# A local-attention and gated-MLP kernel: load order, mask split and written order of its first part

## Chip, cores and metric

The kernel runs on one core of a Trainium2 chip. The metric is the device time of one execution in microseconds (us), the median of several. The core has five engines that each work through a fixed list of instructions: PE (TensorE, with its weight loads listed as PEld), ACT (ScalarE), DVE (VectorE), POOL (GpSimd) and SP (SyncE, which here only issues DMAs). They wait for each other through semaphores.

## What is computed

Attention over 8 batches, 8 heads, 576 positions and 64 channels, in which a query sees 32 keys (the heads of the lower half: the last 32 positions; the others: every fourth of the last 128). Its result, as 4608 tokens of 512 channels, goes through a gated MLP of width 1536. All in float32.

```python
    mask_plain = (rel >= 0) & (rel < window)
    mask_dil = (rel >= 0) & (rel < window * dilation) & (rel % dilation == 0)
    scores = np.where(masks[None, :, :, :], scores, -1000000000.0)
    attn = np.exp(scores - max); attn = attn / (sum + 1e-09)
    x = (attn @ v).transpose(0, 2, 1, 3).reshape(B * S, H * D)
    g = x @ w_gate
    silu = g * (1.0 / (1.0 + np.exp(-g)))
    val = x @ w_val
    return (silu * val @ w_out)
```

## The kernel before

**Two kinds of work.** The tokens are cut into chunks. For the first four chunks of 384 tokens the MLP is done "plain": 12 blocks f of the width 1536 per chunk, and each block is a gate product (`bg`, 12 matmuls of 128x384), a value product (`bv`, 12) and, one block later, the output product (`bo`, 12). Each number is held as a high and a low float32r part, so that a product of 512 channels takes 4 x 3 matmuls, three for the products of the parts. The remaining tokens are done later by another scheme (pieces, line 777), which the change does not touch.

**Packs.** The attention of one chunk and one pair of heads is a pack. Chunk 0 needs packs 0 to 3, all ahead of the first gate product. The stages of a pack have one-letter names in the written order: Q scores on PE (mask by a matmul with the identity, lines 348 and 354), S maximum and subtraction on DVE (368, 369), X exponential on ACT (374), T transposition on PE (378), K copy to SBUF on ACT (384), A products with v on PE (394), N normalisation on DVE (403 to 405), U transposition on PE (412), H high part of x on ACT (444), L low part of x on DVE (448). Packs 4 and on are attended between the products, by a table of slots.

**Weight units.** The weights come as 24 units of 768 KB (two for each f), packed as 64-bit numbers, and each unit passes five stages, written `W0` to `W4`: E on ACT (235), T (253 on ACT or 256 on DVE, as `by_act` says), B on DVE (263 or 266; both read two operands from SBUF), H on ACT (274), L on GpSimd (278). A unit must pass all five before PE can use all of it. The raw units lie in six places, so `w_load` can load a seventh only when B of the first is done.

**Order.** For the first chunk's packs a string of letters sets the order of PE, DVE and ACT word for word (`Y2` is two matmuls that compute nothing and keep PE running, `M` issues two more loads). Behind it the scheduler of the language orders the loop `for s in range(NS)`, in which block s calls the gate product, tanh on ACT (468), a product on DVE (473), the value product, a second product on DVE (478), the high part on ACT (483), the output product of block s-1, and the low part on GpSimd (488). The PSUM banks of the first part are given back before the loop, and `bg` and `bv` take those of `bank_x` and `bank_k`.

**Loads.** SP issues most loads, ACT the masks, pack 1's q and k, and later all v. Each queue issues in the order of the code. The loads take eight semaphores in turn, so a load waits until the one eight places ahead of it has landed.

Of the kernel before, what the change touches and what calls it, by code (L numbers as in the profile page):

```python
# [18 lines left out]
P = 128  # L19
# [116 lines left out]
def attention_moe(ctx, tc, qkb, vb, w, masks, ident, out):  # L136
# [49 lines left out]
    consts = at(0, (NM * BK + P) // 2, BF16)  # L186
    mask_sb, ident16 = consts[:, :NM * BK], consts[:, NM * BK:]

# [5 lines left out]

    WARM = 9
    wt = [at(M_W + 2 * WU * u, 2 * WU, F32R) for u in range(NU)]
# [42 lines left out]
    def by_act(u):  # L239
        return u in (1, 2) or u > 3 and u % 2 == 1  # L240

# [78 lines left out]
    for k, fn, fb in (("qk", FQ, 4), ("v", 4 * FG * (D + 1), 3), ("e", P * FG, 2), ("y", P * FG, 2), ("pt", P * FG, 2)):  # L320
        step = -(-fn // 8) * 8
        early[k] = Ring(fn, *range(o, o + step * fb, step))
        o += step * fb
# [4 lines left out]
    def load_qk(m, pool, engine):  # L328
        t = pool["qk"]()
        engine.dma_start(out=t[:, :pk(m).cols], in_=qkb[m, :, :pk(m).cols])  # L330
        st[m]["qk"] = t
# [184 lines left out]

    bank_x, bank_k, bank_r, *s_banks = [bank(ab, *x) for x in (("fx", 1), ("fk", 1), ("fr", 2), ("fs0", 2), ("fs1", 2))]


    load_qk(0, fa, nc.sync)  # L520
    nc.scalar.dma_start(out=consts, in_=masks)
    load_qk(1, fa, nc.scalar)
    load_v(0, fa, nc.sync)
    nc.sync.dma_start(out=idents, in_=ident.rearrange("n p c -> p n c"))
    nc.vector.memset(ones, 1.0)
# [10 lines left out]

    idle(WARM)
    load_qk(2, fa, nc.sync)
    load_v(1, fa, nc.sync)
    w_load()  # L540
    load_qk(3, fa, nc.sync)
    load_v(2, fa, nc.sync)
    w_load()

    def more_in():
        load_v(3, fa, nc.sync)
        w_load()
        ready["w"] = True

# [6 lines left out]
        "U": lambda m: turn_y(m, x_bank[m]), "H": lambda m: x_copy_hi(m, x_bank[m]),  # L556
        "L": lambda m: x_copy_lo(m, x_bank[m]), "M": lambda m: more_in(), "Y": idle, "W": lambda n: w_one(STAGES[n]),
    }

    et = mybir.EngineType  # L560
    with tc.manual_schedule(engines={et.PE, et.DVE, et.Activation}):
        for what in ("Q0 Q1 Y2 S0 X0 T0 Y2 S1 K0 X1 A0 M0 W0 Q2 N0 T1 K1 S2 X2 Q3 W1 W0 S3 X3 A1 U0 N1 W2 T2 K2 H0 L0 W3 W4 "
                     "T3 A2 K3 W1 U1 N2 A3 H1 L1 W0 W2 U2 N3 W3 H2 U3 L2 W4 H3 L3 W1 W0 W2 W1 W2 W3 W0 W0").split():
            first[what[0]](int(what[1]))
# [33 lines left out]
    def attend(now):  # L598
        what, m = visit.get(now, ("", 0))
        if what == "A":  # L600
            if m > 4:
                results(m - 1, two)
            if m < NPK:
                scores(m, two, m < 8)
            if m > 4:
                norm(m - 1, two, later)
            if m < NPK:
                shift(m, two, later, m < 8)
                exps(m)
                load_v(m, later, nc.scalar)  # L610
                if m + 1 < NPK:
                    load_qk(m + 1, later, nc.scalar)
        elif what == "B":
            if m > 4:
                turn_y(m - 1, two[:, 0])
            if m < NPK:
                turn_e(m, two[:, 1])
                keys(m, two[:, 1], later)
            if m > 4:
                x_copies(m - 1, two[:, 0])  # L620
# [287 lines left out]
def layout(q, k, v, moe_w_gate, moe_w_val, moe_w_out):  # L908
# [17 lines left out]
    w = np.ascontiguousarray(w.reshape(NF, P, 2, WU).transpose(0, 2, 1, 3))  # L926
    masks = np.concatenate([block_masks(), np.eye(P)], axis=1).astype(ml_dtypes.bfloat16)
    order = np.arange(P).reshape(DIL, BQ).T.ravel()
# [21 lines left out]
```

## Time and profile before

| | us |
|---|---|
| median of 3 runs (946.07 to 946.78) | 946.75 |
| the profiled execution | 947.04 |
| its span, first to last instruction | 945.3 |
| PE busy in the span | 929.0 |
| ACT, DVE, POOL busy | 391.9, 633.3, 345.9 |

The prediction is made against the profiled execution, whose span is 945.3 us and whose time is 947.04 us. The trace is read by rows of a timeline: start, length, engine, line, operation, what it writes and reads, how many in a row, and in brackets how long the engine sat idle ahead of it and what ended that. An `x12` row is twelve instructions with no idle time between them. PE's rows overlap, since matmuls are pipelined.

### The profile page before, as it was taken

What the parts mean: (1) busy time and instruction counts of PE and PEld (TensorE: products, weight loads), DVE (VectorE), ACT (ScalarE), POOL (GpSimd) and SP (SyncE); (2) the same over time, 40 slices, a digit from 0 to 9 for tenths busy, and PEclk for the clock granted to TensorE, in tenths of its full rate; (3) what the DMA queues carried; (4) which work ended last, traced back from release to release, by engine and by line L of the source; (5) the groups of instructions that cost most, each with busy time, mean ns of one, the idle gap of its engine ahead of it and who ended that gap; (6) DMA issues with size and microseconds to landing.
All of it is one profiled execution on the core that took longest, in us unless ns stands there. A gap on an engine that the chain in (4) does not pass through costs nothing.

```text
span 945.3 us, 21894 instructions
## 1 busy us (share of the span) xinstructions
PE 929.0 (98%) x9193; PEld 810.9 (86%) x9193; DVE 633.3 (67%) x1008; ACT 391.9 (41%) x687; POOL 345.9 (37%) x364
## 2 busy tenths in 40 slices
PE   7899999999999999999999999999999999999998
PEld 4799999999999999888888788888887888888886
DVE  4767566676677865666568984666689845656882
ACT  4885323233233334343344553343355523334352
POOL 0765421111111131224245672232257723344481
PEclk9999999999999999999999999999999999999999
DMA  9985156577767791776667678776764786655573
GB/s 371 330 282 202 36 200 204 189 235 238 237 196 236 244 324 39 226 245 205 227 205 258 202 241 260 229 235 199 254 203 162 232 256 192 198 185 176 177 249 107
DMA packets 75249, 205.25 MB, mean 217 GB/s; under 512 B 7568, under 2 KB 23824, under 8 KB 75152
## 3 DMA queue, kind: packets, MB, share of 16 engines
q0 software_dynamic: 27216, 99.10, 33.4%
q1 hardware_dynamic: 35696, 65.07, 19.3%
q10 hardware_dynamic: 12240, 39.70, 12.7%
q8 instruction: 72, 1.18, 0.5%
q14 instruction: 25, 0.20, 0.1%
HBM read 161.37 MB, written 42.47 MB: 216 GB/s over the span
## 4 chain that ended last, share of the span: by engine, by line
PE 91%; DVE 4%; DMA 2%; ACT 2%; issue 1%; ACTq 0%; DVEq 0%
PE bo L777 30%; PE bg L777 11%; PE bv L777 11%; PE bo L496 10%; PE bv L459 10%; PE bg L459 10%; PE two L394 3%; PE two L354 2%; PE two L378 2%; DVE at_float L740 2%; PE two L412 1%; DMA at_int<-w 1%; DMA at_float<-qkb 1%; ACT at_float32r L274 0%; DVE at_float L805 0%
## 5 line engine op out<-in xcount | busy, mean ns | idle before, releaser
L777 PE MATMUL bo<-at_float32r 128*128 128x512 f32 x1296 | 308.0, 391 | 0.0
L777 PEld LDWEIGHTS bo<-at_float32r 128*128 128x128 f32 x1296 | 242.1, 188 | 51.6 <-ACT at_float L503 0.2
L706 POOL DMA_DIRECT2D at_float32r<-pieces x189 | 103.5, 548 | 249.7 <-PE bo L777 147.0
L740 DVE TENSOR_TENSOR at_float<-bo,at_float 128x512 f32<-128x512 f32 x168 | 113.8, 686 | 109.6 <-ACT at_float L782 59.8
L488 POOL TENSOR_TENSOR at_float32r<-at_float,at_float32r 128x384 fp32r<-128x384 f32 x48 | 55.4, 1154 | 219.7 <-PE bo L496 179.7
L777 PE MATMUL bv<-at_float32r 128*128 128x512 f32 x486 | 129.7, 393 | 0.0
L777 PE MATMUL bg<-at_float32r 128*128 128x512 f32 x486 | 129.6, 393 | 0.0
L740 DVE TENSOR_TENSOR at_float32r<-at_float,at_float32r 128x512 fp32r<-128x512 f32 (+1 forms) x84 | 99.2, 1205 | 40.5 <-ACT at_float32r L767 24.9
L459 PE MATMUL bg<-at_float32r,at_float32r 128*128 128x384 f32 x576 | 110.9, 339 | 2.1 <-DVE at_float L473 1.3
L740 POOL TENSOR_TENSOR at_float32r<-at_float,at_float32r 128x512 fp32r<-128x512 f32 x63 | 96.4, 1532 | 44.7 <-ACT at_float32r L767 43.3
L459 PE MATMUL bv<-at_float32r,at_float32r 128*128 128x384 f32 x576 | 110.6, 339 | 0.0
L496 PE MATMUL bo<-at_float32r,at_float32r 128*128 128x384 f32 x576 | 110.1, 338 | 0.0
L777 PEld LDWEIGHTS bv<-at_float32r 128*128 128x128 f32 x486 | 90.1, 188 | 19.3
L777 PEld LDWEIGHTS bg<-at_float32r 128*128 128x128 f32 x486 | 90.2, 188 | 19.0 <-DVE at_float32r L740 0.2
L767 ACT CAST at_float32r<-at_float 128x512 fp32r<-128x512 f32 x126 | 76.2, 622 | 68.1 <-PE bv L777 23.2
L459 PEld LDWEIGHTS bg<-at_float32r,at_float32r 128*128 128x128 f32 x576 | 100.0, 188 | 3.8 <-POOL at_float32r L278 1.1
L496 PEld LDWEIGHTS bo<-at_float32r,at_float32r 128*128 128x128 f32 x576 | 100.2, 188 | 0.9
L459 PEld LDWEIGHTS bv<-at_float32r,at_float32r 128*128 128x128 f32 x576 | 100.0, 188 | 1.0 <-DVE at_float L478 0.3
L803 ACT ACTIVATE at_float<-at_float 128x512 f32<-128x512 f32 x72 | 45.6, 633 | 85.4 <-DVE at_float L740 85.2
L473 DVE SCALAR_TENSOR_TENSOR at_float<-at_float,bg 128x384 f32<-128x384 f32 x48 | 26.6, 553 | 76.7 <-ACT at_float L468 76.7
L782 ACT COPY at_float<-bg 128x512 f32<-128x512 f32 x63 | 36.9, 586 | 86.2 <-PE bg L777 86.1
L278 POOL TENSOR_TENSOR at_float32r<-at_int,at_float32r 128x768 fp32r<-128x768 f32 x24 | 45.8, 1916 | 41.5 <-ACT at_float32r L274 41.3
(80 smaller groups left out, 966.3 us busy)
## 6 DMA issues: line engine op xcount, KB each, us to landing
at_float32r<-pieces POOLq DMA_DIRECT2D x189, 512.0 KB, 4.5
pieces<-at_float32r SPq DMA_DIRECT2D x126, 256.0 KB, 4.8
at_int<-w SPq DMA_DIRECT2D x24, 768.0 KB, 6.9
at_float<-vb ACTq DMA_DIRECT2D x28, 390.0 KB, 4.6
at_float<-vb ACTq DMA_DIRECT2D x14, 520.0 KB, 5.5
at_float<-qkb ACTq DMA_DIRECT2D x14, 448.0 KB, 5.5
out<-at_float SPq DMA_DIRECT2D x24, 256.0 KB, 5.3
at_float<-qkb ACTq DMA_DIRECT2D x10, 544.0 KB, 6.7
```

The lines of the kernel that those rows point to most:

```text
L278: nc.gpsimd.tensor_tensor(out=lo, in0=wst.pop(u).bitcast(F32), in1=hi, op=ALU.subtract)
L394: nc.tensor.matmul(out=two[BQ * j:BQ * j + BQ, h, (D + 1) * g:(D + 1) * (g + 1)], lhsT=t[r, BQ * i:BQ * i + BQ], rhs=v[r, i, :], start=Tru ...
L459: nc.tensor.matmul(out=bank[:, :CH], lhsT=wcol(f, o, low), rhs=x[ORDER[j]], start=n == 0, stop=n == len(ops) - 1)
L473: last["h"] = nc.vector.scalar_tensor_tensor(out=t, in0=t, scalar=1.0, in1=bank_g[:, :CH], op0=ALU.add, op1=ALU.mult)
L488: nc.gpsimd.tensor_tensor(out=hl, in0=hst[i][0], in1=hst[i][1], op=ALU.subtract)
L496: nc.tensor.matmul(out=bank_o[j][:, :CH], lhsT=wcol(f, 2 * DM + P * j, low), rhs=x, start=f == 0 and low == 0 and x is hh, stop=f == NF - ...
L706: nc.gpsimd.dma_start(out=taken[asked], in_=pieces[asked % NPIECE])
L740: engine.tensor_tensor(out=out, in0=a, in1=b, op=op)
L767: nc.scalar.copy(out=o[:, 0], in_=src)
L777: nc.tensor.matmul(out=bank, lhsT=w, rhs=x, start=first and n == 0 and t in FRESH, stop=last and n == len(ops) - 1, skip_group_check=True)
L782: nc.scalar.copy(out=kept[KEPT[t]][r], in_=banks[0][r][:, :CS])
L803: nc.scalar.activation(out=f, in_=g, func=AF.Tanh, scale=0.5)
```

## The change

The loads of the start go on SP's queue in a new order: packs 0 to 3 come with their v and the weight units between them. The masks are cut: the identity and the masks of the first packs (576 columns) come first on ACT's queue, the other 320 columns later on SP's. All six raw places are filled without a wait in between (`M` goes). The ring for v gets a fourth place, in memory that is free until the first block's high part is written. Unit 0's T stage goes to ACT, unit 2's to DVE. `bg` and `bv` change places in PSUM. v of pack 4 is loaded by SP behind a weight unit. And the string is written anew.

```diff
-    mask_sb, ident16 = consts[:, :NM * BK], consts[:, NM * BK:]
+    ident16, mask_sb = consts[:, :P], consts[:, P:]
-    WARM = 9
+    WARM = 8
     def by_act(u):
-        return u in (1, 2) or u > 3 and u % 2 == 1
+        return u == 0 or u % 2 == 1
-        early[k] = Ring(fn, *range(o, o + step * fb, step))
+        early[k] = Ring(fn, *range(o, o + step * fb, step), *[M_H + 2 * CH] * (k == "v"))
-    bank_x, bank_k, bank_r, *s_banks = [bank(ab, *x) for x in (("fx", 1), ("fk", 1), ("fr", 2), ("fs0", 2), ("fs1", 2))]
+    bank_k, bank_x, bank_r, *s_banks = [bank(ab, *x) for x in (("fk", 1), ("fx", 1), ("fr", 2), ("fs0", 2), ("fs1", 2))]
+    near = P + 7 * BK
     load_qk(0, fa, nc.sync)
-    nc.scalar.dma_start(out=consts, in_=masks)
-    load_qk(1, fa, nc.scalar)
-    load_v(0, fa, nc.sync)
-    nc.sync.dma_start(out=idents, in_=ident.rearrange("n p c -> p n c"))
+    nc.scalar.dma_start(out=consts[:, :near], in_=masks[:, :near])
+    nc.sync.dma_start(out=idents, in_=ident.rearrange("n p c -> p n c"))
+    load_qk(1, fa, nc.sync)
+    load_v(0, fa, nc.sync)
...
     idle(WARM)
+    w_load()
     load_qk(2, fa, nc.sync)
+    load_qk(3, fa, nc.sync)
     load_v(1, fa, nc.sync)
     w_load()
-    load_qk(3, fa, nc.sync)
     load_v(2, fa, nc.sync)
+    load_v(3, fa, nc.sync)
     w_load()
-
-    def more_in():
-        load_v(3, fa, nc.sync)
-        w_load()
-        ready["w"] = True
+    w_load()
+    nc.sync.dma_start(out=consts[:, near:], in_=masks[:, near:])
+    while w_load():
+        pass
+    ready["w"] = True
...
-        for what in ("Q0 Q1 Y2 S0 X0 T0 Y2 S1 K0 X1 A0 M0 W0 Q2 N0 T1 K1 S2 X2 Q3 W1 W0 S3 X3 A1 U0 N1 W2 T2 K2 H0 L0 W3 W4 "
-                     "T3 A2 K3 W1 U1 N2 A3 H1 L1 W0 W2 U2 N3 W3 H2 U3 L2 W4 H3 L3 W1 W0 W2 W1 W2 W3 W0 W0").split():
+        for what in ("Q0 S0 Q1 Y2 X0 S1 T0 Y2 K0 X1 A0 W1 T1 Y2 N0 K1 Q2 W0 U0 S2 Q3 H0 S3 A1 X2 T2 W2 K2 X3 N1 "
+                     "W0 T3 L0 W3 A2 U1 N2 K3 W4 H1 W1 A3 L1 U2 N3 W0 W2 H2 U3 H3 L2 W3 W1 W0 W4 L3 W1 W2 W2 W3 "
+                     "W0 W4 W3").split():
...
                 exps(m)
-                load_v(m, later, nc.scalar)
+                if m > 4:
+                    load_v(m, later, nc.scalar)
+                else:
+                    with tc.issue_after(last["w"].ins):
+                        load_v(m, later, nc.sync)
...
-    masks = np.concatenate([block_masks(), np.eye(P)], axis=1).astype(ml_dtypes.bfloat16)
+    masks = np.concatenate([np.eye(P), block_masks()], axis=1).astype(ml_dtypes.bfloat16)
```

The instruction lists of the two programs differ in their first part only; from about block 6 or 7 of chunk 0 on they are the same on every engine. Three places show what moved.

The first is ACT's list while the last of the four packs is attended. `L374` is an exponential (the last one of each list is pack 3's), `L384` a copy K, `L235` and `L253` stages of the first two weight units. Before:

```order
L374 ACTIVATE at_384_float_225<-at_384_float_225 128x384
L235 ACTIVATE at_1536_int_150<-at_1536_int_150 128x768
L336 DMA at_1040_float_695<-vb 128x1040
L384 COPY at_384_float_293<-fk 128x384
L374 ACTIVATE at_384_float_215<-at_384_float_215 128x384
L235 ACTIVATE at_1536_int_156<-at_1536_int_156 128x768
L374 ACTIVATE at_384_float_225<-at_384_float_225 128x384
```

Now:

```order
L253 ACTIVATE at_1536_int_145<-at_1536_int_145 128x768
L384 COPY at_384_float_277<-fk 128x384
L235 ACTIVATE at_1536_int_145<-at_1536_int_145 128x768
L444 CAST at_384_float32r<-fx 128x384
L374 ACTIVATE at_384_float_197<-at_384_float_197 128x384
L384 COPY at_384_float_238<-fk 128x384
L374 ACTIVATE at_384_float_230<-at_384_float_230 128x384
L235 ACTIVATE at_1536_int_153<-at_1536_int_153 128x768
```

Unit 1's `L235` stood ahead of pack 3's exponential and now stands behind it; pack 0's `L444` and unit 0's `L253` came in, the load of pack 4's v left.

The second is ACT's list around the tanh of block 0 (`L468`). The `L274` nearest to it is stage H of unit 2. Before:

```order
L444 CAST at_384_float32r<-fs_125 128x384
L253 ACTIVATE at_1536_int_256<-at_1536_int_256 128x768
L235 ACTIVATE at_1536_int_363<-at_1536_int_363 128x768
L468 ACTIVATE at_384_float_572<-bg 128x384
L274 CAST at_1536_float32r<-at_776_int_458 128x768
```

Now:

```order
L444 CAST at_384_float32r<-fs_125 128x384
L274 CAST at_1536_float32r<-at_776_int_416 128x768
L235 ACTIVATE at_1536_int_161<-at_1536_int_161 128x768
L253 ACTIVATE at_1536_int_161<-at_1536_int_161 128x768
L274 CAST at_1536_float32r<-at_776_int_459 128x768
L468 ACTIVATE at_384_float_575<-bg 128x384
```

Both units' stage H now stand ahead of the tanh.

The third is DVE's list around the maximum of pack 4 (`L368`, writes `at_8_float`), which its subtraction `L369` follows; `L263` and `L266` are stage B of weight units, `L473` and `L478` belong to blocks. Before:

```order
L478 SCALAR_TENSOR_TENSOR at_384_float_572<-at_384_float_572,bv 128x384
L368 TENSOR_REDUCE at_8_float_690<-two 128x8
L266 SCALAR_TENSOR_TENSOR at_776_int_458<-at_1536_int_256,at_776_int_458 128x3x256
L369 TENSOR_TENSOR at_512_float_691<-two,at_8_float_690 128x2x4x64
L263 SCALAR_TENSOR_TENSOR at_776_int_324<-at_1536_int_363 128x3x256
```

Now:

```order
L478 SCALAR_TENSOR_TENSOR at_384_float_575<-at_384_float_575,bv 128x384
L266 SCALAR_TENSOR_TENSOR at_776_int_459<-at_1536_int_159,at_776_int_459 128x3x256
L263 SCALAR_TENSOR_TENSOR at_776_int_265<-at_1536_int_161 128x3x256
L368 TENSOR_REDUCE at_8_float_693<-two 128x8
L369 TENSOR_TENSOR at_512_float_694<-two,at_8_float_693 128x2x4x64
```

Both stages B now stand ahead of pack 4's maximum. On ACT, likewise, two `L274` and an `L235` stand ahead of its exponential, where one `L235` and one `L274` stood. On PE, pack 4's transposition stood behind 11 matmuls of block 3's gate product, and its scores within block 1's output product; now its scores stand behind 5 matmuls of block 3's gate product, and the transposition 17 matmuls later.

More of the change, by code (lines that the diff above doesn't have):

```diff
@@ L556, in attention_moe @@
         "U": lambda m: turn_y(m, x_bank[m]), "H": lambda m: x_copy_hi(m, x_bank[m]),
-        "L": lambda m: x_copy_lo(m, x_bank[m]), "M": lambda m: more_in(), "Y": idle, "W": lambda n: w_one(STAGES[n]),
+        "L": lambda m: x_copy_lo(m, x_bank[m]), "Y": idle, "W": lambda n: w_one(STAGES[n]),
     }
```

## Prediction

> **What bounds the kernel now.** First a table of stretches (columns: stretch, length, busy time and count of PE, PEld, DVE, ACT and POOL, granted clock, DMA share, GB/s).
>
> ```profile
> 0.00:5.00 5.00, 4.00 (x11) 1.34 (x11) 0.12 (x2) 1.49 (x2) 0.20 (x4) 1.00 0.63 212
> 5.00:10.00 5.00, 4.31 (x158) 2.69 (x155) 2.36 (x5) 1.42 (x3) 0.00 (x0) 1.00 1.05 416
> 10.00:15.00 5.00, 2.79 (x153) 2.34 (x152) 3.17 (x7) 1.66 (x3) 0.00 (x0) 1.00 1.01 404
> 15.00:19.40 4.40, 1.67 (x46) 1.11 (x52) 2.89 (x7) 2.91 (x6) 0.03 (x1) 1.00 1.03 418
> 19.40:22.80 3.40, 3.40 (x80) 2.61 (x79) 2.41 (x6) 2.46 (x5) 1.71 (x1) 0.50 1.01 416
> 22.80:46.70 23.90, 21.02 (x177) 19.02 (x175) 19.10 (x24) 19.65 (x29) 17.63 (x10) 1.00 0.94 336
> 46.70:520.00 473.30, 473.30 (x5634) 438.31 (x5635) 315.81 (x569) 187.11 (x338) 135.06 (x133) 1.00 0.64 211
> ```
>
> PE is the bound: from 46.70 to 520.00 it has no idle time at all. The change touches only the first part, and the instructions behind it are the same in the same order, so what it can move is PE's time before 46.70. There PE is busy 4.00 + 4.31 + 2.79 + 1.67 + 3.40 + 21.02 = 37.19 us of 46.70: 9.51 us idle. And from 19.40 to 22.80 it is busy at half clock, 3.40 us for 1.7 us of work. So 9.5 + 1.7 = 11.2 us is all that could be won, and the question is which of it goes and what comes back. PE's timeline names the pieces.
>
> ```profile
> 6.95 0.72 PE L354 MATMUL fs<-at_float 64*32 64x64 f32 x48 [0.56 <-DMA at_float<-qkb]
> 7.60 0.60 PE L534 MATMUL fx<-at_float 128*128 128x512 bf16 x2
> ...
> 13.61 0.73 PE L354 MATMUL fs<-at_float 64*32 64x64 f32 x48 [2.21 <-DMA at_float<-qkb]
> ...
> 17.86 0.55 PE L378 MATMUL fs<-at_float,at_float 128*128 128x128 f32 x3 [2.20 <-ACT at_float L374]
> ...
> 19.30 0.62 PE L394 MATMUL fr<-at_float,at_float 64*32 64x65 f32 x23 [0.53 <-issue]
> ...
> 28.19 1.63 PE L459 MATMUL bg<-at_float32r,at_float32r 128*128 128x384 f32 x8 [0.62 <-DVE at_float L473]
> 30.59 0.98 PE L459 MATMUL bg<-at_float32r,at_float32r 128*128 128x384 f32 x4 [0.76 <-POOL at_float32r L278]
> 31.40 2.26 PE L459 MATMUL bv<-at_float32r,at_float32r 128*128 128x384 f32 x12
> 33.50 2.24 PE L496 MATMUL bo<-at_float32r,at_float32r 128*128 128x384 f32 x12
> 36.46 2.38 PE L459 MATMUL bg<-at_float32r,at_float32r 128*128 128x384 f32 x12 [0.72 <-DVE at_float L473]
> ...
> 41.20 0.86 PE L354 MATMUL two<-at_float 64*32 64x64 f32 x64
> ...
> 46.68 0.66 PE L378 MATMUL two<-at_float,at_float 128*128 128x128 f32 x4 [0.78 <-ACT at_float L374]
> ```
>
> In brackets is the idle time and what ended it: pack 1's and pack 3's q and k (6.95, 13.61), pack 3's exponential (17.86), block 1's gate (28.19, 30.59), block 2's (36.46), pack 4's exponential (46.68). With the 1.00 at the start these are 9.38 of the 9.51.
>
> **The change part by part.** Loads first, with KB and us from issue to landing, and the issue of pack 3's q and k.
>
> ```profile
> at_float<-vb SPq DMA_DIRECT2D x4, 390.0 KB, 7.3
> ...
> at_float<-qkb SPq DMA_DIRECT2D x1, 400.0 KB, 8.8
> at_bfloat<-masks ACTq DMA_DIRECT2D x1, 224.0 KB, 4.0
> ```
>
> ```profile
> 4.78 0.33 SPq L330 DMA_DIRECT2D at_float<-qkb  x1
> ```
>
> It landed at 4.78 + 8.8 = 13.6, which is when PE went on. From 5 us on the DMA engines are full (shares 1.05, 1.01), so bytes are time. Ahead of it stood pack 1's v (390 KB), which now comes later, and 224 KB of masks, of which 576 of 896 columns with the identity stay ahead (144 KB): 470 KB less, .48 MB at 416 GB/s, 1.2 us: 12.4. Unit 0 (768 KB) was ahead of it and still is. If the landing lags its bytes less, as pack 1's does early on, it is some 11. PE's own work up to there ends at about 11.7, a little later than before by two filler matmuls (`Y2` stands three times, not twice: 8.04 - 7.60 = .44). So idle there falls from 2.21 to 0 to .9; I take .2: **-2.0**, with **+.4** for the filler. The ninth warm-up matmul lay ahead of the first mask's landing: nothing. Pack 1's q and k: the .56 stays, as a wait of pack 0's transposition for its exponential, since its cover Q1 now stands in front: 0.
>
> Next pack 3's exponential.
>
> ```profile
> 16.49 0.92 ACT L235 ACTIVATE at_int<-at_int 128x768 f32<-128x768 f32 x1 [2.07 <-DMA at_int<-w]
> 17.30 0.51 ACT L374 ACTIVATE at_float<-at_float 128x384 f32<-128x384 f32 x1
> ```
>
> ```profile
> 14.54 0.55 DVE L368 TENSOR_REDUCE at_float<-fs 128x6 f32<-128x384 f32 x1
> 15.12 0.56 DVE L369 TENSOR_TENSOR at_float<-fs,at_float 128x384 f32<-128x384 f32 x1
> ```
>
> Its input was ready at 15.68, but unit 1's L235 stood ahead on ACT and waited for its load until 16.49. That L235 now stands behind it. Pack 3's chain is then: Q3 ends at about 12.5, .2 to the maximum, .58, .56, .51 and one copy ahead on ACT: transposition at about 15.0. PE's other work there ends at about 14. Idle 1.0, and some .5 behind it for the normalisation chain, against 2.20 + .53: **-1.2** (0 if Q3 is as late as before and ACT still full, -2.2 if the chain closes up).
>
> The half clock began at 19.40, after 4.40 us in which PE was busy 1.67. With these waits cut no stretch of 3.4 us has less than half of its time busy: **-1.7** (0 if it returns). [...]
>
> So far -2.0 + .4 - 1.2 - 1.7 = **-4.5**. Behind it PE arrives about 3 us earlier at products whose operands pass five stages on ACT, DVE and GpSimd, and these do not come 3 us earlier.
>
> ```profile
> 26.80 0.49 ACT L468 ACTIVATE at_float<-bg 128x384 f32<-128x384 f32 x1 [0.26 <-PE bg L459]
> ...
> 45.26 0.83 ACT L274 CAST at_float32r<-at_int 128x768 fp32r<-128x768 f32 x1 [1.80 <-DVE at_int L266]
> 46.00 0.63 ACT L374 ACTIVATE at_float<-at_float 128x512 f32<-128x512 f32 x1
> ```
>
> ```profile
> 27.50 0.55 DVE L473 SCALAR_TENSOR_TENSOR at_float<-at_float,bg 128x384 f32<-128x384 f32 x1
> 27.96 0.95 DVE L266 SCALAR_TENSOR_TENSOR at_int<-at_int,at_int 128x768 int32<-128x768 int32 x1
> ...
> 31.65 2.13 DVE L263 SCALAR_TENSOR_TENSOR at_int<-at_int 128x768 int32<-128x768 int32 x1 [0.30 <-ACT at_int L253]
> ...
> 37.65 1.25 DVE L266 SCALAR_TENSOR_TENSOR at_int<-at_int,at_int 128x768 int32<-128x768 int32 x1
> 38.82 1.77 DVE L263 SCALAR_TENSOR_TENSOR at_int<-at_int 128x768 int32<-128x768 int32 x1
> ...
> 43.22 0.54 DVE L478 SCALAR_TENSOR_TENSOR at_float<-at_float,bv 128x384 f32<-128x384 f32 x1
> 43.68 0.68 DVE L368 TENSOR_REDUCE at_float<-two 128x8 f32<-128x512 f32 x1
> ...
> 45.15 0.68 DVE L369 TENSOR_TENSOR at_float<-two,at_float 128x512 f32<-128x512 f32 x1
> ```
>
> ```profile
> 28.09 4.88 POOL L278 TENSOR_TENSOR at_float32r<-at_int,at_float32r 128x768 fp32r<-128x768 f32 x2 [2.67 <-ACT at_float32r L274]
> ...
> 34.62 3.46 POOL L278 TENSOR_TENSOR at_float32r<-at_int,at_float32r 128x768 fp32r<-128x768 f32 x2
> ```
>
> A stage B (L263, L266) takes .95 alone, but 2.13 at 31.65, when GpSimd ran until 28.09 + 4.88 = 32.97: it was held 1.18 of the 1.32 us that GpSimd still had. Begun first (27.96), it takes .95 and GpSimd's pair 4.88 instead of 3.46. [...]
>
> - Block 0's gate: unit 0's last stages and chunk 0's high and low parts are now awaited, two short waits, **+.7** (0 if cover is found, 1.4 if each is as long as block 1's two today).
> - Block 1's gate: unit 2's H (.83) stands ahead of the tanh (.49), which L473 (.55) follows. If its stage B is held, PE has nothing for .83 + .49 + .55 = 1.9, against .62 + .76: **+.5** (-.5 if it isn't held, +1.2 if the hold ends later).
> - Blocks 2 and 3: H, L and the next B of a unit run one behind another when B is held: .83 + 1.73 (half of the pair at 34.62) + .95 = 3.5, 7.0 for a block's two units. PE's 36 matmuls take 3 x (33.50 - 31.40) = 6.3. So .7 to .8 idle for each block: 1.6 against .72, **+.9** (-.7 without the hold, +1.2 with longer ones).
> - Pack 4's transposition: gate 3 starts when L473 is through. From then DVE does T (.95 as B), L478 (.45), two B's now ahead of the maximum (1.25 + 1.77 if held as at 37.65 and 38.82, 1.9 if not), .68, .68, and ACT .63: 6.4 us, 7.0 with half of an L235 (.92) ahead of the exponential. PE meanwhile has 22 matmuls at .175 and the 64 scores (.80): 4.65. Idle 2.4, against .78: **+1.6** (0 to +3).
> - Pack 4's second transposition (L412) comes sooner behind its normalisation: **+.6** (0 to 1; before, the row from 46.70 on has no idle time).
>
> Edits at nothing: the later masks (80 KB) and pack 4's v, for which the first stage that needs them comes over 20 us later; `bg` and `bv` exchanged in PSUM, whose first users end within a microsecond of each other; ACT and DVE exchanging a stage T (.95 on either); pack 1's issue moved off ACT, which idles there. If pack 4's v were late, the wait would be one in its A stage, inside the +.6's bound.
>
> Sum: -4.5 + .7 + .5 + .9 + 1.6 + .6 = **-.2**, so 947.04 - .2 = 946.84; the median stands .29 below the profiled execution: **946.6**.
>
> **Rivals.** *The late waits stay small* (faster). At 27.96 stage B started .13 ahead of GpSimd and was not held. If that is the rule from block 2 on, the cycle per unit is not locked, and blocks 2 and 3, pack 4 cost no more than today: -4.5 + .7 + .5 = -3.3: 943.4. Against it: three of the five B rows quoted are longer than .95.
>
> *A new half-clock stretch* (slower): pack 4's wait. Before 19.40 idle times of 2.20 and .53 near each other brought 1.7 us. From 2.4 us on in one place, which is where my sum puts it, this returns near 46 us: with 3.0 instead of 2.4 idle, +.6 + 1.7 - .2 = +2.1: 948.9. Against it: PE is fully busy on both sides, where before 17.86 it had already stood still.
>
> *The early part does not do what it says*: pack 3's q and k lag as today (Q3 at 13.2) or unit 1 is no earlier. Then -2.8 instead of -4.5: 948.3. For it: 470 KB are all that goes ahead of that load, and it lagged its bytes by some 2 us.
>
> **How the numbers follow.** Forecast .56, faster rival .20, half clock .12, loads not earlier .12. The forecast's own range, from the ends of its terms partly cancelling, is 945.0 to 948.3. Range: 944.0 to 948.9, which reaches most of the way to the faster rival and to the slower one. A measurement of this kernel can tell about 0.2% (1.9 us) from no change: 944.9 to 948.6. Below lie the faster rival and a little of the forecast, .22; above the half clock and part of the last rival, .15; between, .63.
>
> **What would show it.** Idle ahead of pack 3's scores about .2 and ahead of its transposition about 1; no clock of 0.50 near 19 us; block 1's products about 3 us earlier than 28.19; then idle times ended by L473, .8 each, with L263 and L266 rows of 1.7 to 2.1; and 2.4 ahead of pack 4's transposition. Stage B rows of .95 there would be the faster rival. Wrong altogether would be idle time behind 70 us, where nothing moved.

## The result, and the profile after

The changed kernel takes 950.9 us (median of 5 runs, 949.75 to 952.48) against 946.62 for the kernel before: a ratio of 1.0048, 95% interval 1.0033 to 1.0062. It is slower, by .3 to .6%, where no change was forecast. The profiled execution, 949.75 us with a span of 948.0, is the quickest of the five and 2.71 us longer than that of before. The stretches of it, with the columns of the prediction's first table:

```profile
5.00:10.00 5.00, 4.53 (x160) 2.88 (x159) 2.57 (x7) 2.17 (x4) 0.00 (x0) 1.00 1.03 403
10.00:15.00 5.00, 3.55 (x156) 2.68 (x154) 2.47 (x5) 2.30 (x5) 0.00 (x0) 1.00 1.02 410
15.00:19.40 4.40, 2.19 (x58) 1.42 (x56) 2.82 (x9) 2.85 (x6) 1.61 (x1) 1.00 1.03 417
19.40:22.80 3.40, 3.18 (x65) 2.51 (x63) 2.73 (x7) 2.61 (x5) 0.11 (x1) 1.00 1.02 422
22.80:46.70 23.90, 20.28 (x169) 18.16 (x167) 19.81 (x21) 18.08 (x26) 17.10 (x10) 1.00 0.81 309
46.70:97.00 50.30, 47.21 (x588) 44.44 (x587) 34.65 (x50) 35.92 (x56) 31.20 (x20) 1.00 0.69 244
97.00:520.00 423.00, 423.00 (x5033) 390.72 (x5033) 281.56 (x520) 150.56 (x284) 100.59 (x111) 1.00 0.63 208
```

There is no half clock in this execution. Up to 19.40 PE idles less than before, from 22.80 to 46.70 more (23.90 - 20.28 = 3.6 us, where it was 2.9), and from 46.70 to 97.00, where before had none, 3.1 us. Behind 97 us all is as it was. PE's timeline from 11.96 on, the rows with idle time ahead of them and one other:

```profile
11.96 0.72 PE L354 MATMUL fs<-at_float 64*32 64x64 f32 x48 [1.42 <-DMA at_float<-qkb]
...
16.25 0.55 PE L378 MATMUL fs<-at_float,at_float 128*128 128x128 f32 x3 [1.05 <-ACT at_float L374]
17.05 0.43 PE L394 MATMUL fr<-at_float,at_float 64*32 64x65 f32 x24 [0.24 <-DVE at_float L405]
18.39 0.43 PE L394 MATMUL fr<-at_float,at_float 64*32 64x65 f32 x24 [0.92 <-issue]
...
19.87 0.44 PE L459 MATMUL bg<-at_float32r,at_float32r 128*128 128x384 f32 x1 [0.22 <-ACT at_float32r L444]
...
23.37 0.62 PE L459 MATMUL bg<-at_float32r,at_float32r 128*128 128x384 f32 x2 [0.31 <-DVE at_float32r L448]
...
28.45 2.37 PE L459 MATMUL bg<-at_float32r,at_float32r 128*128 128x384 f32 x12 [1.75 <-DVE at_float L473]
30.66 2.24 PE L459 MATMUL bv<-at_float32r,at_float32r 128*128 128x384 f32 x12
...
36.02 2.35 PE L459 MATMUL bg<-at_float32r,at_float32r 128*128 128x384 f32 x12 [1.04 <-DVE at_float L473]
...
43.07 1.16 PE L459 MATMUL bg<-at_float32r,at_float32r 128*128 128x384 f32 x5 [0.53 <-DVE at_float L473]
...
49.99 0.66 PE L378 MATMUL two<-at_float,at_float 128*128 128x128 f32 x4 [1.82 <-ACT at_float L374]
...
63.11 0.66 PE L412 MATMUL two<-at_float,at_float 128*128 128x128 f32 x4 [0.46 <-DVE at_float L369]
...
95.72 0.55 PE L378 MATMUL two<-at_float,at_float 128*128 128x128 f32 x3 [0.81 <-ACT at_float L374]
```

Laid beside the rows of before, the same work stands as follows, after minus before: pack 2's products with v go on at 18.39 instead of 19.30 (-.91); block 1's value product starts at 30.66 instead of 31.40 (-.74, forecast -3.3); by 70 us it is +2.09, and from 105 us on +2.77. So the late part cost 2.83 us, against +3.1 forecast, and some .7 more came at 95 us. What failed is the early part, which won .74 where 3.3 were expected.

### The profile page after: what moved, and what is told of

It reads as the page before. It is cut to its first block, busy times and chain, and to the rows that moved or that the text cites. A ratio compares the mean times of both kernels' runs of the same rounds, so it can differ in the third digit from the quotient of the medians.

```text
span 948.0 us, 21900 instructions
## 1 busy us (share of the span) xinstructions
PE 928.7 (98%) x9194; PEld 809.7 (85%) x9194; DVE 636.8 (67%) x1007; ACT 392.4 (41%) x688; POOL 344.9 (36%) x364
## 3 DMA queue, kind: packets, MB, share of 16 engines
q8 instruction: 72, 1.18, 0.5%
## 4 chain that ended last, share of the span: by engine, by line
PE 86%; DVE 6%; ACT 3%; issue 2%; DMA 2%; SPq 0%; POOL 0%; ACTq 0%; DVEq 0%; POOLq 0%
PE bo L785 30%; PE bg L785 11%; PE bv L785 11%; PE bo L496 9%; PE bv L459 9%; PE bg L459 9%; PE two L394 3%; PE two L354 2%; DVE at_float L748 2%; PE two L378 1%; PE two L412 1%; DMA at_float<-qkb 1%; DMA at_int<-w 1%; DVE at_int L266 1%; DVE at_int L263 1%
## 5 line engine op out<-in xcount | busy, mean ns | idle before, releaser
L473 DVE SCALAR_TENSOR_TENSOR at_float<-at_float,bg 128x384 f32<-128x384 f32 x48 | 26.5, 552 | 72.5 <-ACT at_float L468 72.5
L813 DVE SCALAR_TENSOR_TENSOR at_float<-at_float,at_float 128x512 f32<-128x512 f32 x72 | 52.0, 722 | 10.6 <-ACT at_float L811 10.6
```

The lines of the kernel that those rows point to most:

```text
L473: last["h"] = nc.vector.scalar_tensor_tensor(out=t, in0=t, scalar=1.0, in1=bank_g[:, :CH], op0=ALU.add, op1=ALU.mult)
L813: nc.vector.scalar_tensor_tensor(out=f, in0=f, scalar=1.0, in1=g, op0=ALU.add, op1=ALU.mult)
```

## The experiments

Each time is a median, with the ratio to the kernel before on the same chip in the same job and its 95% interval. The kernel before took 946.96, 947.05, 947.51, 947.32 and 947.71 us in the five jobs, so ratios are compared, not times. One per mille is .95 us.

**Parts undone, first four.** `a1_old_string`: the written order and `by_act` of before, with all the new loads.

```diff
-        return u == 0 or u % 2 == 1
+        return u in (1, 2) or u > 3 and u % 2 == 1
-        for what in ("Q0 S0 Q1 Y2 X0 S1 T0 Y2 ...
+        for what in ("Q0 Q1 Y2 S0 X0 T0 Y2 S1 K0 X1 A0 W0 ...
```

> The changed kernel with the written order and the by_act rule of before; only loads, masks, fourth v place and PSUM exchange stay. Theory A (the loads are right, the new written order gives the time away): pack 3's scores wait until about 12.9 instead of 13.6 us and unit 1 lands .7 earlier, so about .7 us faster than before, 946. Theory B (the loads themselves cost, since unit 0 now lies ahead of pack 2's and 3's q and k): as slow as the changed kernel, 950 to 951.

950.75 us, ratio 1.0035 (1.0022 to 1.0047): not to be told from the change, with the old written order. PE's timeline and a stretch of it show where:

```profile
28.13 1.63 PE L459 MATMUL bg<-at_float32r,at_float32r 128*128 128x384 f32 x8 [0.64 <-DVE at_float L473]
30.53 0.96 PE L459 MATMUL bg<-at_float32r,at_float32r 128*128 128x384 f32 x4 [0.77 <-POOL at_float32r L278]
50.25 0.75 PE L378 MATMUL two<-at_float,at_float 128*128 128x128 f32 x4 [3.54 <-ACT at_float L374]
```

```profile
47.27:50.68 3.41, 0.43 (x5) 0.43 (x5) 2.23 (x3) 1.11 (x2) 0.13 (x1) 1.00 0.93 329
50.68:54.09 3.41, 3.41 (x14) 3.41 (x12) 1.24 (x2) 3.29 (x6) 1.74 (x1) 0.50 0.48 201
```

At block 1 it is where the kernel before is (28.13 and 28.19); then pack 4's transposition waits 3.54 us and half clock follows. Theory B's number came, but not for B's reason. Against the kernel before, only the loads, the cut of the masks, the fourth place for v and the PSUM places differ, and yet the list has pack 4's scores behind six matmuls of block 3's gate (five in the changed kernel; within block 1's output product before). So a change of the loads moved the written order of work 20 us behind them. That the scheduler of the language orders the loop by when it reckons that a load is there is the reading of this; b1 and c2 below, which move a load and with it the list, bear it out.

`a2_w0_later`: unit 0 behind pack 3's q and k.

```diff
-    w_load()
     load_qk(2, fa, nc.sync)
     load_qk(3, fa, nc.sync)
+    w_load()
```

> The changed kernel with unit 0 loaded behind pack 3's q and k, every engine's order as it was. Theory A (the front's delay counts in full): the wait of 1.42 us ahead of pack 2's scores goes, the first product and all behind it come about 1.4 us earlier, 949.5 against 950.9. Theory C (blocks 1 to 3 go at the pace of the weight stages, whatever the front saves): the front is 1.4 us earlier, and the waits ahead of the gates of blocks 1 to 3 grow by as much; 950.5 to 951.5.

951.29 us, ratio 1.0042 (1.0027 to 1.0057): no gain. From its timeline:

```profile
12.39 0.24 PE L348 MATMUL fs<-at_bfloat 128*128 128x192 bf16 x1 [0.41 <-issue]
...
29.82 2.35 PE L459 MATMUL bg<-at_float32r,at_float32r 128*128 128x384 f32 x12 [1.81 <-DVE at_float L473]
37.39 2.35 PE L459 MATMUL bg<-at_float32r,at_float32r 128*128 128x384 f32 x12 [1.05 <-DVE at_float L473]
44.43 1.15 PE L459 MATMUL bg<-at_float32r,at_float32r 128*128 128x384 f32 x5 [0.52 <-DVE at_float L473]
51.35 0.66 PE L378 MATMUL two<-at_float,at_float 128*128 128x128 f32 x4 [1.82 <-ACT at_float L374]
```

Here PE came to block 1 1.37 us later than in the changed kernel, after 6.83 us at half clock (15.56 to 22.39), and the waits behind it are the same to .06 us: 1.81, 1.05, .52, 1.82 against 1.75, 1.04, .53, 1.82. They travel with PE. That speaks against theory C, by which they would shrink when PE comes later. The test is not clean: the half clock took what the front had won, and unit 0's own load is later here. And the wait of 1.42 us for data at pack 2's scores is gone; one "for nothing" came, .41 at 12.39, to which the last group returns.

`a3_l_dve`: stage L of units 2 to 9 by DVE, so that GpSimd's stage L does not hold DVE's stage B (in before, 2.13 us at 31.65 beside GpSimd's pair, .95 alone).

```diff
-        nc.gpsimd.tensor_tensor(out=lo, ...
+        (nc.vector if 2 <= u < 10 else nc.gpsimd).tensor_tensor(out=lo, ...
```

> The changed kernel with stage L of units 2 to 9 on DVE instead of GpSimd. Theory C with the held stage B as its cause: the B rows of these units fall from 1.7 to 2.0 us to .95, the waits ahead of the gates of blocks 1 to 3 (1.75, 1.04, .53) fall by 1.5 to 2.5 us together, 948.5 to 949.5. Rival (DVE's own load is the bound, the hold is a symptom): DVE gets .95 more for each unit and loses about .9 of hold, no change within .5 us, or slower.

949.54 us, ratio 1.0025 (1.0015 to 1.0035). The waits of blocks 2 and 3 go and pack 4's first falls to .51, but block 1's is 2.21 and pack 4's second 1.66 instead of .46. It looked like C2's gain; the last of the L runs below corrects this.

`a5_s4_first`: unit stages ordered behind pack 4's subtraction.

```diff
-        with tc.issue_after(last["h"].ins):
+        with tc.issue_after((last["s"] if s == 2 else last["h"]).ins):
             w_upto(T=W + 5, B=W + 5)
```

> The changed kernel with one stage T and one stage B moved behind pack 4's maximum and subtraction on DVE; PE's order is as it was. Theory D (pack 4's wait of 1.82 us is made by the stages B ahead of its maximum): the wait falls to .3 or less and 1.5 us are won, 949.4. Rival: the unit whose B is moved comes later, and block 4's or 5's gate waits for it instead; 950.5 to 951.

952.57 us, ratio 1.0054 (1.0039 to 1.0069). The wait fell only to 1.14, and pack 4's second transposition now waits 2.36 us, with half clock behind it (the row of twelve value matmuls at 67.45 is 3.72 us long, the one at 30.66 in the changed kernel's profile 2.24): the rival's way, at another place than it named.

**Pack 4, by two edits of its own loads.** `b1_qk4_early` issues its q and k one weight unit earlier:

```diff
-        for what in ("... W4 H1 W1 A3 ...
+        for what in ("... W4 H1 P4 W1 A3 ...
+        "P": lambda m: load_qk(m, later, nc.sync),
-    load_qk(4, later, nc.sync)
     while w_load():
         pass
```

`b2_old_string_qk4` is the same with a1's written order; `d3_v4_only`, `c2_qk4_v4` and `c1_old_string_qk4_v4` put its v back on ACT's queue, alone, with b1 and with b2:

```diff
-                if m > 4:
-                    load_v(m, later, nc.scalar)
-                else:
-                    with tc.issue_after(last["w"].ins):
-                        load_v(m, later, nc.sync)
+                load_v(m, later, nc.scalar)
```

> The changed kernel with pack 4's q and k loaded one weight unit earlier on SP's queue, ahead of unit 9. The language's scheduler then writes pack 4's scores a block earlier, its transposition behind 36 matmuls, and one stage B fewer ahead of its maximum. Theory D2 (pack 4's waits come from its place in the written order, which the order of the loads set): the waits of 1.82 and .46 us at pack 4 go, waits of blocks 1 to 3 (1.75, 1.04, .53) stay; about 2.3 us faster than the changed kernel, 948.5. Rival (stages B that come one later now delay a gate): the waits move to block 3's or 4's gate, 950 to 951.

> The kernel of a1_old_string (written order and by_act of before, new loads) with pack 4's q and k one weight unit earlier. Theory D2: its wait of 3.54 us at pack 4 goes and the half clock behind it with it; what is left are .64 and .77 us ahead of block 1's gate, so 3.5 to 5 us faster than a1_old_string: 945.5 to 947. Rival: the stages B behind come late, as above, 949 to 950.

> The changed kernel with nothing but pack 4's v issued by ACT again. Two separate causes: pack 4's first wait of 1.82 us stays, the .46 at its second transposition and the .81 at 95 us go, 1 to 1.3 us faster than the changed kernel: 949.7. If the place of pack 4's q and k alone decides (one cause), the time is that of the changed kernel, 950.9.

> b1_qk4_early (the new written order) with pack 4's v issued by ACT. Theory E: the waits of 2.16 us at pack 4's second transposition and of .76 at 96 us go; those of blocks 1 to 3 stay (1.98, .26, 1.05); 947.5 to 948, so the new written order stays 1 to 1.5 us behind the old one (c1). Rival: 950.

> b2_old_string_qk4 with pack 4's v issued by ACT again, as in the kernel before. In the written order pack 4's products with v and pack 5's scores then stand one product earlier, and pack 4's second transposition 36 matmuls behind them as in before. Theory E (the move of pack 4's v is what makes pack 4's second transposition wait for pack 5's subtraction): its wait of 2.12 us goes, with a half clock behind it where there was one: about 2 us faster than b2_old_string_qk4, 946 to 946.5. Rival (that wait is DVE's load of stages B and only changes its place): 948.

| | new written order | old written order |
|---|---|---|
| both loads as changed | after: 1.0048 (1.0033 to 1.0062), again 1.0034 (1.0022 to 1.0047) | a1: 1.0035 (1.0022 to 1.0047) |
| q and k earlier | b1: 1.0035 (1.0023 to 1.0046) | b2: 1.0012 (1.0002 to 1.0022) |
| v on ACT | d3: 1.0030 (1.0019 to 1.0040) | |
| both | c2: 1.0008 (.9999 to 1.0017) | c1: .9987 (.9979 to .9996) |

In b1 and b2 pack 4's first wait goes (.29 and nothing), but its second transposition waits 2.16 and 2.12 us for pack 5's subtraction. Their DVE lists still have pack 4's normalisation and pack 5's maximum late (in b2 at 60.03 and 61.06, in c2 at 55.62 and 56.66), by the reading above because the scheduler takes pack 4's v to be late:

```profile
62.26 1.06 PE L412 MATMUL two<-at_float,at_float 128*128 128x128 f32 x4 [2.12 <-DVE at_float L369]
```

In d3 the second wait is gone, and the first stays at 1.84. In c1 and c2 both are gone, but for .31 in c2. No wait at pack 4 is ended by a load in these traces; they end with an exponential or a subtraction, so it is the place in the lists that counts. So they are two causes, but each alone brings little, and neither is clear of the noise: b1 wins 0 to 1.3 per mille, since its second wait grows from .46 to 2.16 us, and d3 .4 to 1.8. Both together win 2.6 to 4.0, which is clear of it (differences to the two measurements of after). That is three quarters of the loss or more.

c1 also beats the kernel before, by 1.3 per mille (.4 to 2.1). What is left between c2 and c1, 2.1 per mille or 2 us, is the new written order itself, with the choice of stages T that goes with it. c1's waits:

```profile
16.63 0.55 PE L378 MATMUL fs<-at_float,at_float 128*128 128x128 f32 x3 [1.66 <-ACT at_float L374]
...
18.81 0.42 PE L394 MATMUL fr<-at_float,at_float 64*32 64x65 f32 x22 [0.78 <-issue]
...
28.17 1.65 PE L459 MATMUL bg<-at_float32r,at_float32r 128*128 128x384 f32 x8 [0.60 <-DVE at_float L473]
30.57 0.96 PE L459 MATMUL bg<-at_float32r,at_float32r 128*128 128x384 f32 x4 [0.75 <-POOL at_float32r L278]
44.19 2.35 PE L459 MATMUL bg<-at_float32r,at_float32r 128*128 128x384 f32 x12 [0.79 <-DVE at_float L473]
```

Block 1 costs 1.35 us and the blocks behind it .79, where c2 has 1.72 and .24 + .31 + 1.04.

**Stage L on DVE, in three more kernels.** `b3_before_l_dve` is a3's edit in the kernel before, `b4_qk4_l_dve` in b1, `c3_qk4_v4_l_dve` in c2.

> The kernel before with stage L of units 2 to 9 on DVE. In the changed kernel this took the waits of blocks 2 and 3 away. Theory C2 (GpSimd's hold costs only where stages B are late already): before has waits of .62, .76 and .72 ahead of gates, of which 1 us could go, but DVE gets more work: 946 to 947, no change. If the hold were the cost of the change as such, the kernel before would win nothing at all.

> b1_qk4_early and stage L of units 2 to 9 on DVE together. If pack 4's place and GpSimd's hold are two separate causes, their gains add: the waits at pack 4, of blocks 2 and 3 go, block 1's stays at about 2: 946.5 to 947.5. If they are one, it is no better than the better of the two (948.5).

> c2_qk4_v4 with stage L of units 2 to 9 on DVE. Theory E with the hold as a cause of its own: block 1's wait of 2 us stays, those of blocks 2 and 3 fall to about 1 together; 946.5 to 947.5. Rival (DVE is full): no gain over c2.

b3 946.89 us, ratio 1.0003 (.9992 to 1.0013); b4 949.62, 1.0023 (1.0014 to 1.0033); c3 948.22, 1.0010 (1.0001 to 1.0018), which is c2's. The hold is real: stages B that took 2.04, 1.75 and 1.80 us in c2 take .95 in c3. But with pack 4 in place taking it away wins nothing: c3 loses c2's .24 and .31, block 1's wait grows from 1.72 to 2.14, another from 1.04 to 1.14, and .69 comes at 93 us. What a3 gained, .9 to 2.3 per mille, then goes rather with pack 4's first wait, which its other DVE order moved; no run takes the two apart.

**The front.** `c4_old_string_qk4_v4_w0` is a2's edit in c1, `d2_x3_first` puts pack 3's exponential ahead of unit 1's E in c4 ("S3 X3 W0" for "W0 S3 X3"), `d1_tanh_first` writes unit 2's H behind the first tanh and unit 3's B behind the product that follows it, in c2:

```diff
-                     "... L3 W1 W2 W2 W3 W0 W4 W3").split():
+                     "... L3 W1 W2 W0").split():
-        w_upto(L=W + 3, H=W + 4, E=W + 6)
+        if s > 0:
+            w_upto(L=W + 3, H=W + 4, E=W + 6)
         gv_mm(ci, f, 0)
         act_tanh(s)
+        if s == 0:
+            with tc.issue_after(last["t"].ins):
+                w_upto(H=W + 3)
+                w_upto(L=W + 3, E=W + 6)
...
+        if s == 0:
+            w_upto(H=W + 4)
         w_upto(L=W + 4, H=W + 5, E=W + 7)
```

> c1_old_string_qk4_v4 with unit 0 loaded behind pack 3's q and k. Theory A (a delay of the front counts in full): the waits of .69 and .73 us at pack 2's and 3's scores go, 1 to 1.4 us faster than c1, 945. Rival (pack 3's exponential behind unit 1's stage E, or unit 0's own stages, come last anyway): no change against c1, or up to 1 us slower.

> c4_old_string_qk4_v4_w0 with pack 3's exponential written ahead of unit 1's stage E on ACT. If that stage E is what the transposition of pack 3 waits for (1.20 to 1.66 us in c1 and c4), the wait falls to about 1.0, the rest of the chain, .3 to .6 us faster than c4, 946. Rival (unit 1's stages come last for block 0): the time moves to the first products, no change.

> c2_qk4_v4 with unit 2's stage H written behind the first tanh on ACT, and unit 3's stage B behind the product that follows the tanh on DVE. Theory F (block 1's gate waits because these two stand ahead): its wait of 1.7 to 2.0 us falls to 1 or less, .8 to 1 us faster than c2: 947.3. Rival G (units 2 and 3 are late in any case): the wait is the same or is ended by stage L on GpSimd, as the .76 in before, and block 2 or 3 waits longer; 948 to 949.

c4 946.53 us, ratio .9990 (.9980 to 1.0000), c1's (one of its eleven executions took 3205.57 us and is not in the ratio); d2 947.77, 1.0009 (1.0000 to 1.0018); d1 948.3, 1.0007 (.9998 to 1.0015), c2's. d1 has .69 ahead of block 1's gate and .33 ahead of block 0's last two value matmuls, where c2 has one wait of 1.72; both are ended by GpSimd's L278, as one is in the kernel before. It won nothing: rival G. d2 cut pack 3's wait from 1.20 to .76 and is no faster than c4, rather slower: its pack 2 then waits 1.07 us for ACT ahead of its products with v, and block 1's gate 1.51, where c4 has .62 and .77. And c4 shows what stands behind the front:

```profile
12.86 0.68 PE L354 MATMUL fs<-at_float 64*32 64x64 f32 x44 [1.08 <-issue]
...
18.99 0.32 PE L394 MATMUL fr<-at_float,at_float 64*32 64x65 f32 x2 [0.69 <-issue]
```

Two stops that the profile gives no releaser for, in the middle of a run of equal matmuls: 222 and 349 matmuls of PE's list stand ahead of them. In the kernels before and after exactly 256 instructions lie between the two places: 127 matmuls, 127 weight loads and two semaphore instructions; the 127 matmuls are the same in c2 and c4. In the traces of before and after a 16 KB transfer of the instruction queue begins at 10.56 and 9.86 us and a second at 16.75 and 15.88, and the 350th matmul starts 1.45 us behind the end of the second (before: 17.85 and 19.30; after: 16.94 and 18.39). In the PE timelines of 19 runs, all but b4's, the 350th matmul comes after such a stop in 16, from .37 us (a1) to 2.03 (d1), and without one in a2, c3 and d3; eight show a stop at the first place, from .17 us (e1) to 1.08 (c4). It is there that a2 waits .41 at 12.39. In the window of 15.8 to 17.0 us of the changed kernel, by the DMA view:

```profile
q1 hardware_dynamic: 91, 0.49, 99.5%
q8 instruction: 1, 0.02, 5.5%
```

This instruction transfer stands among loads that fill the DMA engines (99.5%). Three more runs: `e1_two_places` holds the loads of units 2 and on back until about 16 us, `e2_no_filler` takes the six filler matmuls out, `d4_after_again` is the changed kernel once more.

```diff
-        n = u % 6 if u < NU - NLAST else (u + 2) % 4
+        n = u % 2 if u < 8 else u % 6 if u < NU - NLAST else (u + 2) % 4
```

```diff
-        for what in ("Q0 S0 Q1 Y2 X0 S1 T0 Y2 K0 X1 A0 W1 T1 Y2 N0 ...
+        for what in ("Q0 S0 Q1 X0 S1 T0 K0 X1 A0 W1 T1 N0 ...
```

> The changed kernel with two raw places instead of six for the first eight units, so that units 2 and on are loaded only when B of unit 0 and 1 is done (about 16 us) and the DMA engines have less to do from 14 us. Theory H (PE's 349th matmul waits for an instruction transfer that is queued among the loads): the second 16 KB instruction transfer begins 1 us earlier or more (15 us or less, not 15.9 to 17.3), and the stop of .9 to 1.7 us at the 349th matmul is gone or under .3. Rival I (the transfer begins when PE has used up its instructions, whatever the DMA engines do): transfer and stop stay, at about 16 and 18 us. Behind it the kernel is slower in both cases, 960 or more, since all units come late.

> The changed kernel without its six filler matmuls behind the warm-up. Theory H: the list's place of the stop is counted in instructions, so PE stops after 348 matmuls again, six matmuls of real work later, at the same time of 18 to 19.5 us; filler gone, stop longer, total within .7 us of the changed kernel. If the stop belonged to pack 2's products with v (a wait for data), it would stand at the same matmul of these, number 343.

> The changed kernel itself, to stand beside d1 to d3 on their chip. If half clock makes the difference between its profiled run (949.75, none) and its median (950.9), this run's trace shows one or more stretches of 3.4 us at half clock near 18, 28 or 50 us, and the times spread over 2 to 3 us.

(The matmul that these texts call the 349th is the 350th; 349 stand ahead of it.) e2, 949.95 us, ratio 1.0027 (1.0016 to 1.0039): the stop is behind 349 matmuls again, and so six matmuls of real work later, in the row where 18 of 48 are left:

```profile
18.47 0.38 PE L394 MATMUL fr<-at_float,at_float 64*32 64x65 f32 x18 [1.18 <-issue]
```

So it belongs to a place of the instruction list, not to data: in all 16 timelines with the stop 349 matmuls stand ahead of it. e1, 953.46 us, ratio 1.0073 (1.0046 to 1.0099), where both theories had 960 or more: the DMA engines move 240 GB/s from 16 to 18 us, where the changed kernel has 406, the second transfer begins at 15.48 instead of 15.88 and PE goes on at 17.89 instead of 18.39, but the stop is still 1.14 us. Half a microsecond is less than the two executions of the changed kernel itself lie apart (PE goes on at 18.39 and, in d4, at 19.67). Of theory H the place in the list holds (e2); the transfer a microsecond earlier and the stop under .3 did not come. What sets the time of the second transfer, and whether PE waits for it, is not shown: the traces have the order of the two and the 1.45 us between them.

d4, 950.58 us, ratio 1.0034 (1.0022 to 1.0047): its times spread over 1.04 us, less than expected. Its profiled execution has two stretches of half clock, and ahead of each a stretch in which PE was about half idle (1.60 and 1.96 of 3.42 us):

```profile
3.63:7.05 3.42, 1.82 (x55) 0.84 (x53) 1.11 (x2) 0.03 (x1) 0.00 (x0) 1.00 0.98 314
7.05:10.46 3.41, 3.01 (x55) 1.81 (x55) 1.11 (x2) 0.89 (x3) 0.00 (x0) 0.50 0.99 401
...
17.28:20.70 3.42, 1.46 (x54) 1.11 (x53) 1.08 (x5) 1.37 (x4) 1.72 (x1) 1.00 1.02 412
20.70:24.11 3.41, 3.28 (x57) 2.45 (x56) 2.24 (x6) 2.48 (x4) 0.00 (x0) 0.50 1.01 414
```

## Why the prediction was wrong

**The early part, -4.5: wrong, the step that failed.** It took loads, the exponential and the clock for all that stood ahead of the products. Against the forecast, 2.6 us are missing here in the profile (.74 won at block 1's value product, where 3.3 were expected); the late part, from which most of the loss to the kernel before comes, was priced nearly right.

- Q3, -2.0: measured -.8. Pack 3's own load was forecast at 11 to 12.4 us; it was there before its scores were reached. The wait moved one pack forward, to pack 2's q and k, which now come behind unit 0 and landed at 11.9: PE waited 1.42 us for them. The working counted the bytes ahead of pack 3's load and never those ahead of pack 2's. The third rival had named the 2 us of lag.
- T3, -1.2: the wait itself was forecast at 1.0 and is 1.05, but behind it stood .24 + .92 where .5 was allowed. The .92 is the stop behind 349 matmuls. The row at 19.30 of before, `<-issue`, was read as part of a normalisation chain that would shorten; it is a place of the list where PE stood until 19.30 and now stands until 18.39. Between these two profiles that left the front a gain of .91 us, whatever was saved ahead of it. c4 and d2, which changed the front further and won nothing, go on there at 18.99 and 18.58 after stops of .69 and .53; a2 comes to the place at about 18.6, by its row of 48 from 17.97, at half clock and without a stop. In none of the 19 timelines is it passed before 17.89 (e1). That it is the bound of the front is argued from this, not shown.
- The half clock, -1.7: it went in the profiled execution and not in the usual one. The working took half of 3.4 us busy as the limit, which no run shows as one: half clock followed 1.60 us of idle time in 3.42 in d4, and full clock 1.70 in 3.41 in the changed kernel's profile. The other four of the five runs have a mean clock of .994 to .996, and d4's profiled run, also .996, has two stretches, at 7 and 21 us, against .998 in the profile of before with its one stretch. d4's second stretch comes behind the stop at 349 matmuls, 1.74 us there. But the 108 executions of the kernel before in the five jobs have .994 to .998 too, on average .996: its profile had less half clock than most, and over many executions the change took none away. That is the term's own "0 if it returns"; at pack 4, where the second rival put a new one, both profiles of the changed kernel keep the full clock. How much of the 4.3 us it is can't be told apart run by run; the profiled execution without it is 1.15 us below the median.

The most that the loads won in a run here is c1's 1.3 per mille, 1.2 us, with the old written order and pack 4 put right.

**Block 0, +.7: too small.** The idle time is near the forecast, .22 + .31, but the 24 products take longer in rows that show none: the pair at 23.37 needs .59 until the next row, where two matmuls otherwise need 2 x .175. Their weight loads (PEld) do show waits there, for packs' low parts and a unit's stage H:

```profile
23.37 0.30 PEld L459 LDWEIGHTS bg<-at_float32r,at_float32r 128*128 128x128 f32 x2 [0.59 <-DVE at_float32r L448]
23.96 0.47 PEld L459 LDWEIGHTS bv<-at_float32r,at_float32r 128*128 128x128 f32 x3 [0.29 <-ACT at_float32r L274]
24.70 0.82 PEld L459 LDWEIGHTS bg<-at_float32r,at_float32r 128*128 128x128 f32 x5 [0.26 <-DVE at_float32r L448]
```

From pack 2's second half to block 1's gate PE takes 10.06 us, of which 2.28 idle, against 8.89 of which .62 idle and at most 1.7 the price of the half clock: 7.8 in busy rows against 6.6. So the operands of block 0 came later than PE by more than its idle time tells.

**Block 1, +.5: right size and cause in the trace** (+.37).

```profile
24.56 2.00 DVE L266 SCALAR_TENSOR_TENSOR at_int<-at_int,at_int 128x768 int32<-128x768 int32 x1
26.48 0.95 DVE L263 SCALAR_TENSOR_TENSOR at_int<-at_int 128x768 int32<-128x768 int32 x1
27.84 0.55 DVE L473 SCALAR_TENSOR_TENSOR at_float<-at_float,bg 128x384 f32<-128x384 f32 x1 [0.42 <-ACT at_float L468]
```

```profile
26.59 0.83 ACT L274 CAST at_float32r<-at_int 128x768 fp32r<-128x768 f32 x1 [1.08 <-DVE at_int L266]
27.33 0.48 ACT L468 ACTIVATE at_float<-bg 128x384 f32<-128x384 f32 x1
```

```profile
23.98 1.75 POOL L278 TENSOR_TENSOR at_float32r<-at_int,at_float32r 128x768 fp32r<-128x768 f32 x1 [4.48 <-ACT at_float32r L274]
```

L266 began at 24.56 while GpSimd ran until 25.73 and took 2.00, 1.05 more than alone, of 1.17 that GpSimd had left; then H, tanh and L473 follow, .83 + .48 + .55. d1 adds that taking these two stages out of the way wins nothing, so the order is the way in which the wait shows. Its waits are ended by GpSimd's stage L instead, which points to the units being late; what makes them late no run shows.

**Blocks 2 and 3, +.9: right** (1.04 + .53 against .72, +.85), the stages B held at 1.75 to 2.04. The first rival's time fell with it. (Of the B rows that the prediction shows, three of four are longer than .95, not of five.)

**Pack 4, +1.6 and +.6: right mechanism, too large** (+1.04 and +.46). The stages stand as the working had them:

```profile
44.26 1.80 DVE L266 SCALAR_TENSOR_TENSOR at_int<-at_int,at_int 128x768 int32<-128x768 int32 x1
45.98 1.77 DVE L263 SCALAR_TENSOR_TENSOR at_int<-at_int 128x768 int32<-128x768 int32 x1
47.68 0.68 DVE L368 TENSOR_REDUCE at_float<-two 128x8 f32<-128x512 f32 x1
```

c2 shows that this place, with that of pack 4's v, is most of the loss, which the trace alone could not. a5, with one of the two stages B and a stage T moved behind the subtraction, cut the wait only from 1.82 to 1.14.

**Pack 4's v, +0 "inside the +.6's bound": wrong.** It was priced as a load, by when its data are needed. Its cost was in the written order: with it, pack 4's products with v, and pack 5's maximum, stood later in the lists, 2.1 us where nothing else covered it (b1, b2). From b1 to c2, which differ in this alone, it is 2.7 per mille, 2.6 us.

**Idle behind 70 us** was named as what would make the prediction wrong altogether. It came, .81 us at 95.72, ended by an exponential behind a stage E that waited for unit 23's load (landed 94.3). It is gone in d3 and c2, where v is back on ACT, but also in a3 and e2, where it is not, and in d4, which is the changed kernel itself. So it comes and goes with the execution, and whether the change makes it more frequent is not shown.

## What to carry to other kernels

A load order is also an order of work: where a scheduler places instructions by when it reckons loads to land, moving single loads by one place changed what stood ahead of a maximum 20 us later, and cost more than the loads won. After such an edit the instruction lists behind it are to be compared, and the edits of single loads tried one by one and in pairs, since two waits on one chain hide each other. And the idle time without a releaser that stood behind 349 matmuls in the old written order (.53 us in before) and in the new one (.92 in after) was no wait for data, as e2 shows: 1.18 us at the same count, six matmuls of real work later. What is saved ahead of such a place can be lost in it.

## What the runs showed of the hardware

**The stretches of half clock were 3.41 us long, or twice that.** In before the granted clock is .50 from 19.39 to 22.80 us, in a1 from 50.68 to 54.09, in a3 from 30.40 to 33.81, in d4 from 7.05 to 10.46 and from 20.70 to 24.11, in a2 from 15.56 to 22.39 (6.83). Between d4's two stretches lie 10.24 us, three times 3.41. The first record begins at 5.73 us in before and at 3.92 in after. In the 3.41 or 3.42 us ahead of the half clock PE was idle 2.42 us in before, 2.98 in a1 (above), 2.21 in a3, and 1.60 and 1.96 in d4. But full clock followed 1.84 us of idle time in one place in d3 (ahead of 50.91; the twelve output matmuls from 51.76 took 2.20 us), and 1.70 in the changed kernel's profile, among dense products:

```profile
48.29:51.70 3.41, 1.71 (x11) 1.72 (x12) 2.12 (x5) 3.41 (x7) 2.76 (x2) 1.00 0.89 298
```

So in these traces the idle time alone does not decide; what does is open. d4 has two stretches of half clock, the other profile of the same kernel none. That a wait can cost 1.7 us more (half of 3.41) in one execution and nothing in another is the author's estimate from these rows; it fits times of one kernel that spread over up to 5 us here (c4: 945.36 to 950.52).

**PE stopped at a fixed count of its instruction list**, behind 349 matmuls, for .37 to 2.03 us in 16 of 19 timelines, and in before and after went on 1.45 us behind the end of a 16 KB transfer of the instruction queue. The loads fill the DMA engines there in the changed kernel (share .99 from 16 to 18 us, 406 GB/s); in e1, where they move 240 GB/s, it stops as well, 1.14 us.
